# Two 256 KB weight loads, each cut into sixteen transfers of eight rows that lie four partitions apart

## The chip, the cores and the metric

One core of a Trainium2 chip runs the kernel. The metric is the device time of one execution in microseconds (us), given as the median of several runs. A "load" below is one of the kernel's DMA transfers from HBM to SBUF, "packets" are the pieces in which the trace records DMA work, "the lower engines" are those eight of the core's sixteen DMA engines that carry the eight-row transfers (in the changed kernel eight chains of packets, with 160 packets of 2 KB each), and "the upper engines" the other eight (there 128 each). The trace numbers no engine; the texts call the two groups 0 to 7 and 8 to 15.

## The reference, cut to what matters

Two attention blocks for one new token are computed and laid side by side. B is the larger: 4 batches, 32 heads, 8192 cached keys and values of 128 elements in bfloat16.

```python
def _B_ref(x, k_cache, v_cache, wq, wo):
    q = (x @ wq) ...                                   # one query per batch and head
    scores = jnp.einsum("bhqd,bhkd->bhqk", q, k_cache) * (Dh ** -0.5)
    p = _softmax(scores, axis=-1)
    o = jnp.einsum("bhqk,bhkd->bhqd", p, v_cache)
    return o.transpose(0, 2, 1, 3).reshape(B, Sq, H * Dh) @ wo
...
return jnp.concatenate([a, b], axis=-1)
```

Each key and value is used once, so some 587 MB must be read for little arithmetic.

## The kernel before

All loads but the two small inputs are issued by SyncE, in a fixed order, each after a wait that says its buffer is free. B's output weights come in 16 loads of two heads each (`hp`), 128 partitions of 2 KB. Their one buffer `wos` is filled anew after the products with the old contents are done.

```python
def dma_wos(hp):
    src = B_wo[2 * hp * P:2 * (hp + 1) * P, :].rearrange("(p r) n -> p (r n)", r=2)
    sch.add_dma("sp", lambda e: e.dma_start(wos[:, :, :].rearrange("p r n -> p (r n)"), src), "d_wos",
                waits=[("fin", NCA + 4 * hp - 1)] if hp else [], key=("wos", hp))
# ... (cut: dma_kv, which issues one 4 MB load of keys or values, 128 partitions of 32 KB)
for kind, c in loads:
    if kind == "k" and c >= NCA and (c == NCA or (c - NCA) % 4 == 3 and c > NCA + 3):
        dma_wos((c - NCA) // 4)
    dma_kv(kind, c)
    # ... (cut: SyncE tells TensorE by a semaphore that wos has landed; A's weights)
```

`add_dma` raises the load's semaphore by 16 when it has landed; one load on sixteen engines gets one increment from each engine (the trace has 16 for the last load and, per load, one 4-byte packet in each of sixteen chains). The last value load is cut in five pieces, so that TensorE can start on it early.

## Time and profile before

| | before |
|---|---|
| median, 6 runs | 1374.13 us (1373.97 to 1374.33) |
| profiled span | 1372.6 us |
| moved | 587.53 MB, mean 428 GB/s |
| TensorE busy | 86% of the span |
| DMA queue 1, packets | 25208, 99.8% of 16 engines' time |

The kernel is bound by its DMA engines, and the prediction below shows the lines. What matters beyond the mean is that a load has landed only when the last of its engines has finished, and that the engines are not level: the sixteen increments of the last load are 3.6 us apart, and TensorE starts on it at 1369.10, just after the last of them (1369.06).

### The profile page before, as it was taken

How to read it: one execution, taken by the hardware profiler on the slowest of the kernel's cores; microseconds unless marked ns; L12 is line 12 of the kernel's file. 1: busy time of each engine (PE TensorE's matmuls, PEld its weight loads, DVE VectorE, ACT ScalarE, POOL GpSimd, SP SyncE). 2: the span in 40 equal slices, each digit the busy share in tenths (PEclk: the TensorE clock that was granted, in tenths of full speed). 3: DMA queues.
4: the chain of work that ended last, by engine and by line, in shares of the span. 5: the costliest groups of instructions: out<-in, count | busy, mean ns of one | idle time of the engine just before them, and what ended most of it. 6: DMA issues, size and time to landing. Idle time of an engine off the chain costs nothing.

```text
span 1372.6 us, 59967 instructions
## 1 busy us (share of the span) xinstructions
PE 1176.5 (86%) x27065; PEld 1132.9 (83%) x27067; DVE 656.6 (48%) x1434; ACT 434.7 (32%) x650; POOL 7.3 (1%) x28
## 2 busy tenths in 40 slices
PE   4888898889888888988888888888898888888888
PEld 4777898888888888888888878888898888888888
DVE  1775454445444444454445444444454444444544
ACT  1553232333223322332233323322333233323322
POOL 2000000000000000000000000000000000000000
PEclk9998999999999999999999999999999999999999
DMA  9999999999999999999999999999999999999998
GB/s 400 423 424 432 429 433 428 433 432 432 432 431 433 429 434 428 434 430 434 430 434 430 430 433 432 432 431 433 429 433 431 434 429 434 430 432 432 432 427 352
DMA packets 25261, 587.53 MB, mean 428 GB/s; under 512 B 2820, under 2 KB 2840, under 8 KB 6296
## 3 DMA queue, kind: packets, MB, share of 16 engines
q1 hardware_dynamic: 25208, 587.22, 99.8%
q8 instruction: 16, 0.26, 0.1%
q14 instruction: 5, 0.04, 0.0%
q10 hardware_dynamic: 32, 0.01, 0.0%
HBM read 587.21 MB, written 0.01 MB: 428 GB/s over the span
## 4 chain that ended last, share of the span: by engine, by line
DMA 65%; PE 33%; issue 1%; DVE 1%; ACT 0%; SPq 0%; DVEq 0%
DMA kv<-in_B_k_cache_dram 57%; PE tr L408 21%; PE sc L410 9%; DMA kv<-in_A_k_cache_dram 5%; DMA kv<-in_B_v_cache_dram 3%; PE po L410 2%; PE fin L410 1%; PE ms L410 0%; ACT kt L476 0%; DVE sA L527 0%; SPq L365 0%; ACT pba L597 0%; PE ms L408 0%; DVE zA L683 0%; DVE rm L536 0%
## 5 line engine op out<-in xcount | busy, mean ns | idle before, releaser
L408 PE MATMUL tr<-identb,kv 128*128 128x128 bf16 x8704 | 697.9, 230 | 148.8 <-DMA kv<-in_B_k_cache_dram 141.5
L478 DVE COPY kt<-tr 128x1024 bf16<-128x1024 bf16 x736 | 502.6, 690 | 457.1 <-PE tr L408 452.7
L408 PEld LDWEIGHTS tr<-identb,kv 128*128 128x128 bf16 x8704 | 552.9, 104 | 165.2 <-DMA kv<-in_B_k_cache_dram 81.7
L476 ACT ACTIVATE kt<-tr 128x1024 bf16<-128x1024 bf16 x352 | 359.3, 1023 | 666.8 <-PE tr L408 666.7
L410 PE MATMUL sc<-qb,kt 128*128 128x64 bf16 x8704 | 446.2, 196 | 14.3 <-ACT kt L476 12.8
L410 PEld LDWEIGHTS sc<-qb,kt 128*128 128x128 bf16 x8704 | 366.4, 100 | 26.0 <-ACT kt L476 20.2
L410 PE MATMUL po<-pbb,kv 128*128 128x64 bf16 x8320 | 284.4, 192 | 4.5 <-issue 3.9
L410 PEld LDWEIGHTS po<-pbb,kv 128*128 128x128 bf16 x8320 | 263.2, 97 | 7.1 <-issue 4.1
L577 ACT ACTIVATE pbb<-sc,negb 64x128 bf16<-64x128 f32 x128 | 51.6, 403 | 254.3 <-DVE negb L564 253.5
L541 DVE TENSOR_REDUCE rm<-sc 64x1 f32<-64x128 f32 x128 | 37.0, 289 | 56.6 <-PE sc L410 55.7
L553 DVE TENSOR_REDUCE gm<-ms 1x2 f32<-1x128 f32 (+1 forms) x72 | 20.1, 279 | 48.4 <-PE ms L408 48.4
L564 DVE COPY negb<-ms 128x1 f32<-128x1 f32 (+1 forms) x72 | 11.4, 158 | 47.0 <-PE ms L410 46.8
L410 PE MATMUL ms<-identf,gx 1*128 1x1 f32 (+1 forms) x144 | 27.2, 256 | 0.8 <-DVE zA L683 0.8
L666 DVE TENSOR_TENSOR oz<-po,rz 128x8 bf16<-128x8 f32 x33 | 5.5, 166 | 40.7 <-PE po L410 40.7
L410 PEld LDWEIGHTS ms<-identf,gx 1*128 1x128 f32 (+1 forms) x144 | 21.1, 182 | 4.6 <-DVE zA L683 0.9
L577 ACT ACTIVATION_READ_ACCUMULATOR pbb<-sc,negb 64x1 f32 x128 | 23.7, 185 | 0.0
L410 PE MATMUL po<-pba,kv 128*128 128x64 bf16 x512 | 20.5, 199 | 3.5 <-issue 2.1
L410 PEld LDWEIGHTS po<-pba,kv 128*128 128x128 bf16 x512 | 17.9, 102 | 5.7 <-ACT pba L597 4.2
L408 PE MATMUL ms<-identf,rm 128*1 128x128 f32 (+1 forms) x72 | 19.5, 271 | 2.4 <-DVE rm L536 2.3
L557 DVE TENSOR_SCALAR gx<-gm 1x128 f32<-1x128 f32 (+1 forms) x72 | 16.0, 222 | 2.5
L683 DVE CAST zB<-ms 64x8 bf16<-64x8 f32 x64 | 10.5, 164 | 9.2 <-PE ms L410 8.7
L410 PE MATMUL ms<-xT,kv 128*128 128x4 bf16 x256 | 7.1, 166 | 8.8 <-DMA kv<-in_A_wq_dram 5.0
(61 smaller groups left out, 173.9 us busy)
## 6 DMA issues: line engine op xcount, KB each, us to landing
kv<-in_B_k_cache_dram SPq DMA_DIRECT2D x63, 4096.0 KB, 26.5
kv<-in_B_v_cache_dram SPq DMA_DIRECT2D x63, 4096.0 KB, 30.9
kv<-in_A_k_cache_dram SPq DMA_DIRECT2D x8, 2048.0 KB, 14.8
kv<-in_A_v_cache_dram SPq DMA_DIRECT2D x8, 2048.0 KB, 16.2
kv<-in_A_wq_dram SPq DMA_DIRECT2D x1, 4096.0 KB, 12.5
kv<-in_B_wq_dram SPq DMA_DIRECT2D x1, 4096.0 KB, 27.1
wor<-in_A_wo_dram SPq DMA_DIRECT2D x8, 512.0 KB, 9.8
wos<-in_B_wo_dram SPq DMA_DIRECT2D x16, 256.0 KB, 20.3
```

The costliest lines, as they stand in the source:

```text
L408: sch.add("pe", lambda e: e.transpose(o, l, r), waits, key)
L410: sch.add("pe", lambda e: e.matmul(o, l, r, start=start, stop=stop), waits, key)
L476: sch.add("act", lambda e: e.activation(dst, src, ACTF.Copy), waits=waits, key=("ev", s))
L478: sch.add("dve", lambda e: e.tensor_copy(dst, src), waits=waits, key=("ev", s))
L541: sch.add("dve", lambda e, src=src, pp=pp: e.tensor_reduce(out=rm[pp, m, 0:1], in_=src, axis=AX.X, op=ALU.max), waits=[("S", ch["s_last"]) ...
L553: sch.add("dve", lambda e: e.tensor_reduce(out=gm[0:C, m, 0:U], in_=src, axis=AX.X, op=ALU.max), waits=[("trm", c)], key=("gmax", c))
L557: sch.add("dve", lambda e: e.tensor_scalar(out=dst, in0=gv, scalar1=-scale, scalar2=None, op0=ALU.mult), waits=[("gmax", c)], key=("gx", c))
L564: sch.add("dve", lambda e: e.tensor_copy(negb[:, m, 0:C], ms[:, col:col + C]), waits=[("bc", c)], key=("negb", c))
L577: sch.add("act", lambda e, src=src, pp=pp, n=n, u=u: e.activation(probs_of(c)[pp, :, u], src, ACTF.Exp, bias=negb[pp, m, 0:1], scale=scale ...
L666: sch.add("dve", lambda e: e.tensor_tensor(out=o, in0=i0, in1=i1, op=ALU.mult), waits=waits, key=("oT", c))
L683: sch.add("dve", lambda e, src=src, pp=pp: e.tensor_copy(z[pp, :].rearrange("p (r b) -> p r b", r=k), src), waits=[("sm", c)] + free if h ...
```

## The change

Its intent, as far as the code tells: if an eight-row transfer runs on eight of the sixteen engines only, always the same ones, each of the two loads takes work off the upper engines and gives it to the lower ones, to level the sixteen. No run had shown this when the prediction was made; it was the author's assumption, and the packets of the changed kernel bear it out (160 and 128 of 2 KB, below).

```diff
+EIGHTS = (1, 2)
 ...
             src = B_wo[2 * hp * P:2 * (hp + 1) * P, :].rearrange("(p r) n -> p (r n)", r=2)
-            sch.add_dma("sp", lambda e: e.dma_start(wos[:, :, :].rearrange("p r n -> p (r n)"), src), "d_wos",
-                        waits=[("fin", NCA + 4 * hp - 1)] if hp else [], key=("wos", hp))
+            dst = wos[:, :, :].rearrange("p r n -> p (r n)")
+            waits = [("fin", NCA + 4 * hp - 1)] if hp else []
+            if hp in EIGHTS:
+                for i in range(16):
+                    rows = slice(32 * (i // 4) + i % 4, 32 * (i // 4) + i % 4 + 29, 4)
+                    sch.add_dma("sp", lambda e, rows=rows: e.dma_start(dst[rows, :], src[rows, :]), "d_wos",
+                                waits=waits, key=("wos", hp) if i == 15 else None)
+                return
+            sch.add_dma("sp", lambda e: e.dma_start(dst, src), "d_wos", waits=waits, key=("wos", hp))
```

## The prediction

The forecast's sum is -0.2 us, 1373.9 us. Its split of the work, "engines 0 to 7" with 16 rows each and "engines 8 to 15" with none: take that split as the author's assumption.

> **What bounds the kernel now.** I read the page's slice rows first, to see which resource is never idle, then the DMA queues, then the chain that ended last.
>
> ```profile
> DMA  9999999999999999999999999999999999999998
> GB/s 400 423 424 432 429 433 428 433 432 432 432 431 433 429 434 428 434 430 434 430 434 430 430 433 432 432 431 433 429 433 431 434 429 434 430 432 432 432 427 352
> ...
> q1 hardware_dynamic: 25208, 587.22, 99.8%
> q8 instruction: 16, 0.26, 0.1%
> q14 instruction: 5, 0.04, 0.0%
> ...
> DMA 65%; PE 33%; issue 1%; DVE 1%; ACT 0%; SPq 0%; DVEq 0%
> ```
>
> The 16 DMA engines are full from first slice to last, at about 432 GB/s; one queue's packets fill 99.8% of 16 engines' span, and the chain of waits is DMA for 65%. TensorE is 86% busy but waits for keys: in the view of waits,
>
> ```profile
> PE tr L408 <- DMA kv<-in_B_k_cache_dram: 141.5, 58, 4.1
> ```
>
> that is 58 times, 141.5 us in total. So bytes bound the kernel. More exactly, the slowest of the 16 engines does, since a load has landed only when each engine has done its share. The end shows it:
>
> ```profile
> 1366.64 2.12 PEld L410 LDWEIGHTS po<-pbb,kv 128*128 128x128 bf16 x56
> 1366.85 2.03 PE L410 MATMUL po<-pbb,kv 128*128 128x64 bf16 x56
> 1369.10 0.29 PEld L410 LDWEIGHTS po<-pbb,kv 128*128 128x128 bf16 x8 [0.35 <-DMA kv<-in_B_v_cache_dram]
> 1369.11 0.41 PE L410 MATMUL po<-pbb,kv 128*128 128x64 bf16 x8 [0.23 <-DMA kv<-in_B_v_cache_dram]
> ```
>
> The last eight value tiles start when their transfer lands at 1369.06, and the program ends 3.5 us later (1372.6).
>
> **The sixteen engines are not level.** The trace's semaphore records give the 16 increments of that last transfer: nine at 1365.47 to 1367.44, seven at 1368.40 to 1369.06, a spread of 3.6 us. The packet records (start, duration, size; no engine number) say why. On one engine a packet starts 4 to 5 ns before the one before it ends, so I followed 16 chains, holding each to the known order of loads: eight packets of each size, then one 4-byte semaphore write, 1575 queue-1 packets per chain. Durations are regular (32 KB 1.213 us, 2 KB 0.084 us), and the chains split cleanly. The 15 instruction fetches of 16 KB before 168 us (queue 8, 19.67 to 167.14 us) go round robin over eight chains: seven get two, one gets one. A fetch takes about 1.0 us and the 32 KB packet behind it 1.7 instead of 1.21, so it costs its engine about 1.5 us. These seven chains end at 1367.97 to 1368.64; the one with a single fetch at 1366.81. The other eight have the small input and output packets (queue 10) and five 8 KB fetches: six end at 1364.90 to 1365.47, two, with two 8 KB fetches each, at 1366.26 and 1366.99. The skew is complete by about 170 us and then stands still: 3.9 us after 400 packets per chain, 3.7 at the end.
>
> [...]the four-row output of the first problem has four packets at 127.92 to 128.81, on chains without 16 KB fetches[...].
>
> **The change, part by part.** The second and third loads of B's output weights (hp 1 and 2) become 16 transfers each.
>
> *Work per engine.* Packets follow one another in 80 ns for 2 KB and about 6 ns for a semaphore write. Before, one load costs an engine 8 x 80 + 6 = 646 ns (a chain's 644 to 647 ns agree). After, engines 8 to 15 have none: -0.646 us per load, -1.29 for two. Engines 0 to 7 have 16 rows and 16 semaphore writes: 16 x 86 = 1.376 us, +0.73 per load, +1.46 for two. If the fetch chains are 8 to 15, the worst late one ends at 1368.64 - 1.29 = 1367.35, the worst early one at 1366.99 + 1.46 = 1368.45. The maximum falls from 1368.64 to 1368.45: **-0.2 us**. The other early ones end near 1366.9; so up to 1.3 us would be won if that one chain were not so laden, but nothing unloads it.
>
> *Issues on SyncE.* The timeline of the issuing queue:
>
> ```profile
> 206.56 0.33 SPq L374 DMA_DIRECT2D kv<-in_B_k_cache_dram  x1
> 211.92 0.33 SPq L374 DMA_DIRECT2D kv<-in_B_v_cache_dram  x1
> 220.08 0.33 SPq L340 DMA_DIRECT2D wos<-in_B_wo_dram  x1
> 223.35 0.33 SPq L374 DMA_DIRECT2D kv<-in_B_k_cache_dram  x1
> 228.69 0.33 SPq L374 DMA_DIRECT2D kv<-in_B_v_cache_dram  x1
> ```
>
> Issues without a wait between them stand 0.474 us apart (the last value pieces, 1328.18, 1328.65, 1329.13). Sixteen take 16 x 0.474 = 7.6 us, from 220.08 to 227.7. The key load that went at 223.35 goes about 4 us late; the value load at 228.69 waits for TensorE anyway. By the chains, each engine had 17 to 21 packets in hand at 220.08; less 7.6 / 1.21 = 6, engines 8 to 15 still have 11 at least, 13 us of work. So the delay is hidden: 0. The same at 298.45, where the distances are the same.
>
> *Sequencer fetch.* Thirty more instructions on SyncE. Its 8 KB fetches come 128 instructions apart in my count (460 and 1333 us); they come earlier, but stay two: 0.
>
> *Sum:* -0.2 us, 1374.1 - 0.2 = 1373.9.
>
> **Rivals.** *A. Wrong half:* if the fetch chains are not just engines 8 to 15, a laden engine gets +1.46 and the end moves to 1370.1, so about 1375.5. Against it: the early group holds the four-row transfers and is eight chains, as is the other. I give it a tenth. *B. Semaphore writes cost more than 6 ns* when one follows every packet, as nothing in this trace does; 30 ns more on 32 writes is +1 us on engines 0 to 7, so 1374.9. For it: only the untested alternation. Against it: after eight packets the next one starts at once. A fifth. *C. A full queue:* the last issue took 6.12 us (at 1329.92), with 77 to 81 packets in hand per engine, so there is a limit. If it counted transfers, not packets, SyncE would stand still among the sixteen until about 240, engines 8 to 15 would run dry for some 4 us, twice: 1380 or more. Against it: that issue was let go at 1336.04, when no transfer landed in full, and in the change an engine holds at most about 60 packets. A twentieth. *D. Everything fits and the laden early chain is lucky:* -1.2 us, 1372.9.
>
> **Range and chances.** A and B push up by 1 to 1.5 us, D down by 1.2; the three runs before lie within 0.4 us. So 1372.8 to 1375.6 should hold it 8 times in 10. All of this is 0.1%; 2% is 27 us, which only a stall of rival C, several times over, would reach. Faster 0.005, same 0.985, slower 0.01.
>
> **What would show each step.** In the changed profile: issues of output weights 46 instead of 16 (14 + 32), queue-1 packets up by 2 x (16 x 8 - 16) = 224 to 25432; the issue blocks of about 7.6 us at 220 and 298; no dip in the DMA row there; the spread of the last transfer's increments down from 3.6 us to about 1.6, and its last increment near 1368.9. A spread of 5 us would be rival A; late increments in the eight small-packet chains with a longer gap after each semaphore write, B; SyncE issues of several us at 220, with a dip in the slices after, C. The prediction is wrong if the end moves by more than the spread can give, or if the DMA row dips.

## The result, and the profile after

| | before | after |
|---|---|---|
| median, 6 runs each | 1374.13 us | 1379.38 us (1379.16 to 1379.75) |
| ratio | 1 | 1.0039 (95% interval 1.0026 to 1.0051) |
| profiled span | 1372.6 us | 1377.7 us |
| queue-1 packets | 25208 | 25432 |
| last load's increments | 1365.47 to 1369.06 us | 1367.25 to 1374.20 us |

The ratio is the mean time of the changed kernel's fast runs over that of the other's fast runs of the same rounds, so not quite the ratio of the medians. By the 2% rule the two are the same; the difference of 5.25 us is nevertheless far outside the spread of either, and outside the predicted range.

Rows of the page after, against the same rows in the prediction's first fence:

```profile
DMA  9999999999999999999999999999999999999997
GB/s 400 423 425 432 428 431 419 424 431 407 434 430 433 431 431 431 431 432 431 433 430 433 429 432 433 429 433 430 435 429 432 431 430 433 428 435 431 433 428 328
...
q1 hardware_dynamic: 25432, 587.22, 99.6%
...
DMA 61%; PE 35%; DVE 1%; issue 1%; ACT 1%; SPq 0%; DVEq 0%
```

The DMA row still stands at 9. But the rate has fallen in the slices that hold 220 to 250 us and 310 to 330 us (each is 34 us long): 419 and 424 in the seventh and eighth, 407 in the tenth. The engines are as busy as before and move less. A view by stretches makes it plain; its last two columns are the DMA engines' busy share and the rate. First the kernel before:

```profile
236.00:244.00 8.00, 8.00 (x174) 8.00 (x172) 5.29 (x10) 3.07 (x3) 0.00 (x0) 0.92 1.00 426
316.00:324.00 8.00, 7.80 (x182) 7.68 (x179) 5.14 (x10) 4.09 (x4) 0.00 (x0) 1.00 1.05 445
```

Then the changed one:

```profile
236.00:244.00 8.00, 7.80 (x196) 7.68 (x193) 5.14 (x10) 3.35 (x4) 0.00 (x0) 1.00 1.03 344
316.00:324.00 8.00, 7.80 (x183) 7.68 (x181) 5.32 (x10) 4.10 (x4) 0.00 (x0) 1.00 1.04 356
```

In the two stretches in which the cut loads are carried out, full engines move 344 and 356 GB/s instead of 426 and 445. (The view counts a packet whole in the stretch in which it starts, so a share can be a little over 1 and a rate a few per cent off.) A packet that takes longer counts as busy all the same, so the busy share cannot show this loss.

The issuing queue after:

```profile
222.00 10.85 SPq L348 DMA_DIRECT2D wos<-in_B_wo_dram  x16
232.89 0.44 SPq L384 DMA_DIRECT2D kv<-in_B_k_cache_dram  x1
233.37 0.44 SPq L384 DMA_DIRECT2D kv<-in_B_v_cache_dram  x1
242.27 0.33 SPq L384 DMA_DIRECT2D kv<-in_B_k_cache_dram  x1
```

The sixteen issues take 10.85 us, 0.67 us apart, and the key load goes at 232.89. The end after, in order of time:

```profile
1374.24 0.29 PEld L420 LDWEIGHTS po<-pbb,kv 128*128 128x128 bf16 x8 [0.35 <-DMA kv<-in_B_v_cache_dram]
1374.25 0.41 PE L420 MATMUL po<-pbb,kv 128*128 128x64 bf16 x8 [0.23 <-DMA kv<-in_B_v_cache_dram]
```

The tail has the same form as before, only 5.14 us later: TensorE starts on the last eight tiles when the last transfer has landed, 1374.20 against 1369.06.

**The packets.** I followed the sixteen chains of packets through the changed kernel in the same way as in the prediction. Eight chains carry 160 packets of 2 KB and eight carry 128, as two cut loads on eight of the engines should give (144 + 16 and 144 - 16). No chain has a gap of more than 50 ns from 3 us to the end of its last load. What is new is slow packets: between 235 and 247 us, 54 packets of 32 KB take over 1.3 us, up to 2.37, against none in the kernel before (1.213 to 1.25), and 40 of the 128 packets of 2 KB take over 0.1 us, up to 0.26, against none. Between 314 and 328 us it is 56 and 44. Added up over all packets of both sizes, the time above 1.213 and 0.084 us is 27.4 + 28.2 = 55.6 us of engine time, against 1.1 + 1.2 before: 3.3 us for each of sixteen engines. Outside these stretches the packets are as before. Everything that has to be explained lies in two stretches of some 9 us (237.4 to 246.5 and 318.4 to 327.7), from the time at which the rows of a cut load are carried. All sixteen chains are slowed: the sums of single chains over both stretches are 2.8 to 3.5 us for the eight that carry nothing of the cut loads and 3.4 to 4.5 us for the eight that carry them.

### The profile page after: what moved, and what is told of

It is laid out like the page before. It is cut to its first block, busy times and chain, and to the rows that moved or that the text cites. A ratio compares the mean times of both kernels' runs of the same rounds, so it can differ in the third digit from the quotient of the medians.

```text
span 1377.7 us, 59997 instructions
## 1 busy us (share of the span) xinstructions
PE 1175.4 (85%) x27065; PEld 1132.8 (82%) x27067; DVE 656.7 (48%) x1434; ACT 435.2 (32%) x650; POOL 7.4 (1%) x28
## 3 DMA queue, kind: packets, MB, share of 16 engines
q1 hardware_dynamic: 25432, 587.22, 99.6%
## 4 chain that ended last, share of the span: by engine, by line
DMA 61%; PE 35%; DVE 1%; issue 1%; ACT 1%; SPq 0%; DVEq 0%
DMA kv<-in_B_k_cache_dram 56%; PE tr L418 22%; PE sc L420 9%; DMA kv<-in_B_v_cache_dram 3%; PE po L420 2%; DMA kv<-in_B_wq_dram 2%; PE fin L420 1%; DMA kv<-in_A_k_cache_dram 1%; PE ms L420 1%; DVE sA L537 1%; ACT kt L486 0%; ACT pba L607 0%; DVE rm L546 0%; SPq L375 0%; DVE sA L535 0%
## 5 line engine op out<-in xcount | busy, mean ns | idle before, releaser
L420 PE MATMUL ms<-identf,gx 1*128 1x1 f32 (+1 forms) x144 | 27.4, 257 | 0.8 <-DVE zA L693 0.8
```

The lines of the kernel that those rows point to most:

```text
L420: sch.add("pe", lambda e: e.matmul(o, l, r, start=start, stop=stop), waits, key)
```

## The experiments

All outputs are right. "Slowed" in the table is that sum over both stretches, for 32 KB and 2 KB packets (512 B packets are left out); before it is 2.3 us. The differences are to the median of the kernel before in the same rounds (7 runs each, 6 for the changed kernel).

| run | the loads of hp 1 and 2 | median, us | difference | slowed, us |
|---|---|---|---|---|
| changed kernel | 16 transfers of 8 rows | 1379.38 | +5.25 | 55.6 |
| e1_two_parts | 120 and 8 rows | 1376.93 | +2.56 | 53.8 |
| e2_level_many | 8 transfers of 16 rows | 1376.04 | +1.67 | 30.2 |
| e3_extra_small | whole, 15 extra of 512 B rows, all partitions | 1378.55 | +4.18 | 36.7 |
| e4_six_parts | 5 of 24 rows, one of 8 | 1377.14 | +2.77 | 44.6 |
| f1_extra_low | whole, 15 extra to partitions 0 to 63 | 1378.62 | +4.44 | 31.3 |
| f2_extra_high | whole, 15 extra to 64 to 127 | 1379.16 | +4.98 | 44.2 |
| f3_two_halves | 64 and 64 rows | 1377.26 | +3.08 | 47.7 |
| f4_columns | 4 transfers of 128 rows, 512 B of each | 1374.73 | +0.55 | 5.3 |
| g1_four_low | whole, 4 extra of 2 KB rows to 0 to 31 | 1374.44 | +0.24 | 2.4 |
| g2_four_high | whole, 4 extra of 2 KB rows to 64 to 95 | 1375.69 | +1.49 | 22.1 |
| g3_one_load | 16 of 8 rows, hp 1 only | 1376.62 | +2.42 | 27.3 |
| h1_sixteen_low | whole, 16 extra of 2 KB rows to 0 to 63 | 1378.96 | +4.86 | 17.8 |

### First four: semaphore writes, or unlevel work

Theory S was that 128 semaphore writes per load clog something shared. Its rival U was a bundle: unlevel work, and rows written to partitions that, as the author supposed, other engines write in whole loads.

```diff
-for i in range(16): ... rows = slice(32 * (i // 4) + i % 4, 32 * (i // 4) + i % 4 + 29, 4)
+cuts = [slice(0, 120), slice(120, 128)]                                              # e1_two_parts
+cuts = [slice(64 * (i // 4) + i % 4, 64 * (i // 4) + i % 4 + 61, 4) for i in range(8)] # e2_level_many
+cuts = [slice(24 * i, min(24 * i + 24, P)) for i in range(6)]                        # e4_six_parts
```

```diff
 if hp in EIGHTS:                                                                     # e3_extra_small
+    for i in range(15):   # the same eight rows each, 512 B of them, to a tile that nobody reads
+        ... e.dma_start(spare[rows, :], src[rows, 0:256]) ... "d_wos"
-    return
 sch.add_dma("sp", lambda e: e.dma_start(dst, src), "d_wos", waits=waits, key=("wos", hp))
```

> Theory S: the many one-row transfers, each row with a semaphore write behind it (128 writes per load from eight engines), clog something that all sixteen engines share; the unlevel load costs only its own work. Here each of the two loads is cut in 120 and 8 rows: still all 16 rows per engine on the lower eight, but two semaphore writes per engine. S expects no slowed 32 KB packets and an end moved by the work alone, the laden lower chain 1368.21 + 1.29, so about 1375.0 us. Rival U: the unlevel load itself (eight engines out of step with the others, rows written across to the upper partitions) slows all. U expects the time of the changed kernel, about 1379.4 us, with slowed 32 KB packets after both loads.

> Level and many: eight transfers of 16 rows per load, one row and one semaphore write per engine and transfer on all sixteen engines, again 128 data rows and 128 semaphore writes per load, but every engine has its eight rows as before. S expects bursts of slowed packets and about 1378 us (the 4 us of slowed packets of the changed kernel, without the work moved). U expects no loss beyond 7 semaphore writes of 6 ns: 1374.1 to 1374.3 us.

> The two loads stay whole as in the kernel before; 15 extra transfers of eight rows of 512 B each go to a spare tile beside each. Work added on the lower engines 15 x about 36 ns x 2 = 1.1 us, so by work alone about 1374.7 us. S expects 1378 to 1379 us with slowed 32 KB packets of all engines beside the extra transfers; U expects 1374.7 us.

> Five transfers of 24 rows and one of 8: the unlevel work in full, 48 semaphore writes per load instead of 128. S expects between 1375.0 us (if there is a threshold above 48) and 1376.2 us (if the loss is proportional to semaphore writes: 4 us x 32/112 on top of 1375.0). U expects about 1379.4 us.

Measured: 1376.93, 1376.04, 1378.55 and 1377.14 us. First a correction: e1 and e4 were not the cuts that their expectations describe. Each engine that takes part in a transfer writes one semaphore packet (4 bytes; the changed kernel has 224 more of them than the 2804 before, which is 2 x (16 x 8 - 16)), and the data packets are as many as before, so the packets of queue 1 tell how many engines took part. In e1 and then in e4:

```profile
q1 hardware_dynamic: 25222, 587.22, 99.8%
q1 hardware_dynamic: 25312, 587.22, 99.8%
```

Against the 25208 before, these are 7 and 52 more per load: 23 semaphore writes in e1 and 68 in e4, not 16 and 48. So the 120 rows ran on 15 engines (15 + 8 = 23) and each 24 rows on 12 (5 x 12 + 8 = 68), which the expectations overlooked. If each transfer is shared out evenly, and always among the same engines, then in e1 eight engines had 9 rows, seven had 8 and one had none; in e4 they had 11, 10 (four engines) and none (four). Neither has "the unlevel work in full", so their forecasts rest on a wrong sum.

Neither theory fits all four (e3 alone lies in the range of S). With two transfers (e1) and 23 semaphore writes per load the slowed time is about as large as in the changed kernel, 53.8 us, so many semaphore writes are not needed for it. The engine of e1 that carries nothing of the cut loads is slowed too, by 3.2 us over both. With work that is level by design (e2: 16 rows a transfer for sixteen engines, taken as one row each; no packet count of it is given here) there are still 30.2 us of it, so unlevel work is not needed either. The issues are not needed: in e1 the two of them took 0.73 us and the key load went at 223.04, as before. Only the other half of U is left.

### Second four: whose partitions, and rows against columns

Theory P: a row written to a partition that another engine serves in whole loads slows them all. No trace here names the partitions that an engine writes, so this "serves" stays the author's assumption, as do rows "written across" in the expectations. What the runs can show is to which partitions eight-row transfers may write without slow packets: f1 writes to 0 to 63, f2 to 64 to 127.

```diff
 if hp in EIGHTS:                                                                # f1_extra_low, f2_extra_high
+    for i in range(15):   # spare is [P, 512] here; base = 0 or 64
+        r0, x = base + 32 * (i // 4 % 2) + i % 4, slice(256 * (i // 8), 256 * (i // 8) + 256)
+        rows = slice(r0, r0 + 29, 4)
+        ... e.dma_start(spare[rows, x], src[rows, x]) ... "d_wos"
-    return
 sch.add_dma("sp", lambda e: e.dma_start(dst, src), "d_wos", waits=waits, key=("wos", hp))
```

```diff
+cuts = [slice(0, 64), slice(64, 128)]                                           # f3_two_halves
+for i in range(4): ... e.dma_start(dst[:, x], src[:, x]), x = 256 columns each  # f4_columns
```

> The first four runs showed slowed packets with 16 semaphore writes as with 128, so theory S has lost its first leg. New theory P: what clogs is a row that is written to a partition which another engine serves in the whole loads (rows of the upper 64 partitions written by the lower engines[...]). Here the two loads stay whole; 15 extra transfers of eight 512 B rows go to partitions 0 to 63 only, four apart[...]. P expects no slowed packets and only the added work of 1.1 us on the lower engines, at most 1375.3 us. S (many small transfers with semaphore writes) expects the time of the run with 15 extra transfers over all partitions, 1378.5 us.

> As the run before it, but all 15 extra transfers go to partitions 64 to 127[...]. P expects slowed packets of all engines and at least the 1378.5 us of the run whose extra rows lay half and half. S expects 1378.5 us, the same as for the lower partitions.

> Two transfers of 64 rows per load: four rows per engine and transfer on all 16 engines, level, two semaphore writes per engine, two issues.[...] P expects slowed packets after both loads and 1375 to 1376.5 us, as for the level run with eight transfers (1376.0). S and every theory of unlevel work expect 1374.3 us, as before.

> Four transfers of all 128 rows, 512 B of each, per load: [...]level, 64 semaphore writes per load, four issues. P expects no slowed packets and the time before, 1374.4 us (plus at most 0.3 us for smaller packets). S expects 1375 to 1377 us.

Measured: 1378.62, 1379.16, 1377.26 and 1374.73 us. The pair f3 and f4 speaks for P: two transfers of half the partitions cost 3.08 us, four transfers of all partitions and a quarter of each row 0.55 us, although f4 has twice the issues. P had the sizes only roughly: f3 came about 0.8 us above its range, and in f4 16 packets of 32 KB per stretch still took up to 1.35 us. The stretch view of f3, whose last two columns are again busy share and rate:

```profile
236.00:244.00 8.00, 7.80 (x195) 7.68 (x193) 5.02 (x9) 3.54 (x4) 0.00 (x0) 1.00 0.99 344
```

And of f4, which has nearly the 426 GB/s of the kernel before:

```profile
236.00:244.00 8.00, 8.00 (x177) 8.00 (x175) 5.33 (x10) 3.07 (x3) 0.00 (x0) 0.94 1.03 422
```

The runs taken as level also let the slowed packets be turned into time: in f3 they are (47.7 - 2.3) / 16 = 2.8 us per engine and the time rose by 3.08; in e2 (30.2 - 2.3) / 16 = 1.7 us and it rose by 1.67.

But f1 contradicts P: extra rows on partitions 0 to 63, for which it expected 1.1 us of work and at most 1375.3 us, cost 4.44 us, as S had said. Its packets look different, though. In f1 only 8 packets of 32 KB per stretch are slow (1.7 to 2.0 us), by their number one for each of eight engines, and all other 32 KB packets took at most 1.25 us. In f2, where the rows went to partitions 64 to 127, 32 and 36 are slow. Long in f1 are also 24 packets of 2 KB, 0.32 to 0.81 us each, of the whole load that follows the fifteen pairs of a 512 B row and a semaphore write. So the engines that did the many one-row transfers stall at their end, and the others run on. That is a second cause, called S2 in the next expectations. The semaphore records fit: in f1 up to 83 semaphore packets per us are sent while at most 45 increments per us arrive, and the lag from packet to arrival grows from some 0.5 us to 2.8; in the kernel before it is at most 0.58.

### Third call: each cause alone

```diff
 if hp in EIGHTS:                                   # g1_four_low, g2_four_high
+    for i in range(4):                             # spare is [P, 1024]; base = 0 or 64
+        rows = slice(base + i, base + i + 29, 4)
+        ... e.dma_start(spare[rows, :], src[rows, :]) ... "d_wos"
-    return
 sch.add_dma("sp", lambda e: e.dma_start(dst, src), "d_wos", waits=waits, key=("wos", hp))
```

```diff
-EIGHTS = (1, 2)                                    # g3_one_load
+EIGHTS = (1,)
```

> The run with 15 extra small transfers to the lower partitions left all upper engines at full speed but stalled the lower ones after their row-and-semaphore pairs. So two causes now: P (rows written to partitions that another engine serves slow all engines) and S2 (a long run of one-row transfers, each with its semaphore write, stalls the engine that does them). Here only four extra transfers of eight 2 KB rows[...]: more bytes per engine than in the 15 extra ones (8 KB against 7.5 KB), but 4 semaphore writes instead of 15. Work 4 x 86 ns x 2 = 0.7 us on the lower engines. S2 expects 1374.3 to 1374.9 us and no slowed 32 KB packets; if bytes or the 8-row form cause the stall, 1378 us.

> As the run before it, with the four extra transfers to partitions 64 to 95[...]. Same bytes, same number of semaphore writes, same issues. P expects slowed 32 KB packets on most engines and about 1 us more than its twin (half as many rows written across as in the changed kernel). If partitions do not matter, the same time as its twin.

> The changed kernel with only the second load (hp 1) cut up. If both loads cost the same, independently: half of +5.2 us, so 1376.8 us, with slowed packets near 240 us only. If the cost is in something else than the loads themselves (the late key and value issues, the end of the program), not half.

Measured: 1374.44, 1375.69 and 1376.62 us. All three fell where the two causes put them. The twins g1 and g2 differ in nothing but the partitions that four extra transfers write and the rows of the source that belong to them: the issues take 2.84 us in both, with the same bytes, rows per engine and semaphore writes. The stretch view of g1:

```profile
236.00:244.00 8.00, 7.80 (x196) 7.68 (x193) 5.13 (x10) 3.36 (x4) 0.00 (x0) 1.00 1.02 430
```

And of its twin g2, at the same busy share:

```profile
236.00:244.00 8.00, 7.80 (x197) 7.68 (x193) 5.13 (x10) 3.37 (x4) 0.00 (x0) 1.00 1.01 393
```

On partitions 0 to 31 the extra rows leave no slow packet at all and cost 0.24 us, the work that they add. On partitions 64 to 95 33 and 34 packets of 32 KB are slow and the run takes 1.25 us longer. This pair shows the part of P that a run can show, that it matters to which partitions such rows go, with two limits. That rows to 64 to 95 do harm because other engines write these partitions in whole loads was not shown. Also, in every run a partition is written from the source row of the same number, so that it is the writing and not the reading of these rows that slows the engines is argued and was not tested. And g1 has more bytes per engine than f1 (8 KB against 7.5) with 4 transfers instead of 15, and no stall: the number of transfers makes S2, not the bytes. (f1's rows are also shorter; the last run below, with rows as long as g1's, stalls too.)

The third run cut only the first of the two loads. The rates show the loss where it was cut and none at 316 us, where the slowed packets sum to 1.2 us as in the kernel before:

```profile
236.00:244.00 8.00, 7.93 (x186) 7.81 (x182) 5.32 (x11) 4.02 (x4) 0.00 (x0) 1.00 1.03 348
316.00:324.00 8.00, 7.86 (x184) 7.74 (x180) 5.32 (x10) 4.09 (x4) 0.00 (x0) 1.00 1.00 426
```

It costs 2.42 us, near half of 5.25. So each load brings its own loss.

### The last: how large the stall is at the changed kernel's pace

```diff
 if hp in EIGHTS:                                   # h1_sixteen_low
+    for i in range(16):                            # spare is [P, 2048]; each of the 8 row sets twice
+        r0, x = 32 * (i // 4 % 2) + i % 4, slice(1024 * (i // 8), 1024 * (i // 8) + 1024)
+        rows = slice(r0, r0 + 29, 4)
+        ... e.dma_start(spare[rows, x], src[rows, :]) ... "d_wos"
-    return
 sch.add_dma("sp", lambda e: e.dma_start(dst, src), "d_wos", waits=waits, key=("wos", hp))
```

> How much of the changed kernel's stall on the lower engines does the run of 16 row-and-semaphore pairs make by itself, with 2 KB rows as there (the 15 extra transfers had 512 B rows, so pairs every 35 ns; here every 86 ns)? The two loads stay whole[...]. Work alone: 16 x 86 ns x 2 = 2.75 us on the lower engines, from about 1368.2 to 1370.95, so about 1376.5 us. If pairs stall an engine also at this pace, by 1.7 us per load as with 512 B rows, about 1379.9 us. No slowed packets on the upper engines in either case.

Measured: 1378.96 us, between the two. Eight packets of 32 KB per stretch are slow again, up to 2.02 us, one in each chain that carries the extra rows; the other 32 KB packets are not. The pairs themselves run at 84 ns per row at first; the first slow one starts 1.21 us after the first pair of any engine, time for 14 pairs, and most of those behind it take 0.16 to 0.21 us. The slowed time is 8.7 + 9.1 us, less 2.3 as before, on eight engines: 1.9 us per lower engine, or 0.95 per load. With the work of 2.75 us that gives about 1378.4; half a microsecond is not accounted for.

No version beat the kernel before, and nothing in the runs points to one: half of the rows of such a cut load go to partitions 64 to 127, and of the twins g1 and g2 the one that writes there is the dearer.

## Why the prediction was wrong

Its reading of the kernel stood: the slowest of sixteen DMA engines sets the end, the skew comes from the instruction fetches, eight-row transfers go to eight engines, the late issues are hidden. The sign and size of the change did not.

**"Before, one load costs an engine 646 ns. After, engines 8 to 15 have none: -0.646 us per load."** This is the step that failed most. It treats an engine's time as its own, so that work taken off it is time won. In the changed kernel the upper chains with two fetches end at 1369.7 to 1370.2 (two chains that cross cannot always be told apart), and the five before with fetches at the same times ended at 1367.97 to 1368.64: later by about 1.3 to 2.1 us instead of earlier by 1.29. They had less to do, and their remaining packets were slowed. In place of the step the runs showed that rows of eight-row transfers to partitions 64 to 95 come with slow packets (g2: 33 and 34 of 32 KB, against none in g1 on 0 to 31), and that in the changed kernel all sixteen chains are slowed, the eight that carry nothing of the cut loads by 2.8 to 3.5 us. The mistake was to count how many rows an engine has and not where they go: half of each cut load's rows lie in partitions 64 to 127. Why rows there make slow packets was not shown. An estimate from the packets says only that it is more than the time of the rows: in g2 the four extra rows per lower engine, 0.34 us of writing, would, if all engines waited for them, delay 16 engines by 0.34 us each, 5.5 us per load; the slowed time above its twin's is (22.1 - 2.4) / 2 = 9.9 us. Why it is more stays open. So does which rows an engine takes of a transfer of 24, 64 or 120; the packet counts, printed for e1 and e4, say only how many engines take part.

**"16 x 86 = 1.376 us, +0.73 per load" for the lower engines.** As work this holds: in g1, where nothing else happens, 0.69 us of added work moved the end by 0.24 us, as its expectation had it. But a run of sixteen one-row transfers also stalls its engine. That is the place of rival B, which the prediction gave a fifth and +1 us in all; h1 has about 0.95 us per load, 1.9 for both. Rival B's mechanism, a semaphore write that takes more than 6 ns, is not what the packets show: semaphore packets still take 9 to 27 ns, while the 2 KB packets and the next 32 KB packet take the time. The lag from semaphore packet to arrival reached 2.3 us in the changed kernel, against at most 0.58 before; what makes it was not shown. Whether the semaphore writes or the one-row transfers as such make the stall was not separated; each such transfer here carried one.

**"If the fetch chains are 8 to 15".** They are not, so rival A held too. In the changed kernel's chains most fetches lie in the eight chains with 128 packets of 2 KB, but a chain with 160 has those at 59 and 161 us and ends last of all, at 1373.72. The run with one cut load is cleaner: its two last chains, 1370.75 and 1371.10, both have 152 packets of 2 KB, so they are lower engines, and fetches at 52 and 154, and at 59 and 162 us. Two of the eight fetch engines are lower ones. For one of them the prediction's own sum should have been 1368.21 + 1.46 = 1369.67 instead of 1368.45, a loss of 1.0 us over 1368.64 rather than a gain of 0.2.

**The sum, mended.** From 1369.67 the last chain went to 1373.72, 4.05 us later. Its slowed packets add up to 4.5 us, 4.3 above the 0.14 of a chain before, so slowing accounts for this part within 0.3 us. Together with the 1.03 us from rival A it is 5.08 us, against the 5.14 us by which the last landing moved. P has most of the 4.05: the upper chains, without a single one-row transfer, were slowed by 3.1 us on average and the lower ones by 3.9. The lower engines' own stall would then be about 0.8 us, less than the 1.9 us of h1, so the two causes do not simply add; why is open.

**"So the delay is hidden: 0."** Right in its result, wrong in its size. An eight-row issue takes 0.67 us from one to the next, not 0.474, so 10.85 us instead of 7.6, and the value load was late too. Still no chain ran dry. Rival C did not occur: SyncE was never held for several us by one of the sixteen.

**"The spread down to about 1.6 us."** It rose to 7.0 us. **"No dip in the DMA row"** was a poor sign: there was none, and the loss was there nevertheless, in the rate. The counts of issues (46) and packets (25432) were right.

## What to carry to other kernels

In a DMA-bound kernel, look at the rate beside the busy share, since engines with slowed packets stay fully busy (here at 344 instead of 426 GB/s). If a load that covers all 128 partitions must be cut while others run, cut it along its columns and not along its rows: here that was +0.55 us (f4) against +3.08 (f3). Before moving work from one engine to another, ask which resource it takes along: here the destination partitions stayed where they were, and the move cost more in slowed packets than it took off.

## Measured by the way

- Two transfers of 64 rows in place of one of 128 cost 1.54 us per load (f3, 3.08 us for two), and 16 of eight rows 2.6 us (the changed kernel, 5.25 us for two).
- 33 and 34 packets of 32 KB took up to 1.74 us instead of 1.21 when four eight-row transfers went to partitions 64 to 95 (g2), none when they went to 0 to 31 (g1).
- A single semaphore write is a 9 ns packet. A run of 15 or 16 one-row transfers with one each stalled its engine by about 0.95 us (2 KB rows, h1) and 1.8 us (512 B rows, f1, (31.3 - 2.3) / 16).
- The interval between issues on SyncE goes with the form of the transfer: 0.474 us for 128 rows (the last value pieces before), 0.41 for 24 neighbouring rows (e4), 0.63 for 16 rows four apart (e2), 0.67 for eight rows four apart.
- The DMA engine that fetches 16 KB of instructions loses about 1.5 us, and fifteen fetches fell on eight of the sixteen in turn, two of them lower ones. Fetches of 8 KB occur too; two of them, at 460 and 1333 us before, lie 128 SyncE instructions apart.
